# One exponential for the first half, the second half's scores earlier, and V's units regrouped in a segment-recurrent attention

## Chip, cores and metric

The kernel runs on one core of one Trainium2 chip. The metric is device time in microseconds (us) of one execution. Three runs of the kernel before gave 795.5, 796.58 and 797.68 us; the median, 796.58, is the time before.

## The reference

A gated sum of two branches over 2048 tokens of width 512, in bf16. Branch B is layer norm, a GELU layer of 1376 and a projection back. Branch A is attention over segments of 32 tokens, each with 8 memory tokens in front, 32 heads of 128; the first 8 output rows of one segment are the memory of the next, so the 64 segments are a chain:

```python
for s in range(n_seg):                       # 64
    h = jnp.concatenate([mem, x[:, 32*s:32*s+32]], axis=1)      # 40 rows
    q, k, v = (jnp.einsum('btd,dhe->bhte', h, W) for W in (Wq, Wk, Wv))
    scores = jnp.einsum('bhqe,bhke->bhqk', q, k) * scale
    p = _softmax(jnp.where(mask, scores, -1e9), axis=-1)
    o = jnp.einsum('bhqk,bhke->bhqe', p, v)
    o = jnp.einsum('bhte,hed->btd', o, Wo)
    mem = o[:, :8]
    outs.append(o[:, 8:])
return g * a + (1 - g) * b                   # g = sigmoid((x * gate_w).sum(-1))
```

## The kernel before

A first stage (lines 292 to 545, about 100 us) computes branch B and loads the weights of branch A. Then the loop of line 626 runs the 64 segments s = 4 T + si, T being a tile of 128 tokens. The order of every engine's instructions is written out by hand; nothing is rescheduled, and each engine works through its own list in order, waiting on the others by semaphores.

TensorE works in groups of four matmuls that sit side by side on the array, 32 columns each. A group with 512 columns of weights streaming past is called a unit here. hT holds the segment's input, transposed: the 8 memory rows and 24 of the segment's tokens. The remaining 8 tokens of each of the four segments of a tile ("left") have no dependence on memory and are projected one tile ahead, in side units that are spread over the segments to fill TensorE's pauses.

One segment, in TensorE's order:

1. Q and K from hT: 16 units (L110) into the PSUM banks U[0..3]; ScalarE casts each bank to Tb (L115), VectorE transposes it into QT or KT (L119). U[0] and U[1] give the first half of the heads, U[2] and U[3] the second.
2. scores of the first half (L256, L260) into the bank SbF, on top of a mask written earlier (L248). ScalarE takes the exponentials (L661) into E in two pieces: 16 of 56 columns per group, then 40. The 16 hold the memory rows' queries, the 40 the others.
3. four V units into X1 (L129), copied by ScalarE to V (L676); one V unit into X2; msum(0): the sums of the memory queries of the first half (L267, L270) into a corner of U[0]; VectorE takes the reciprocal (L668) and multiplies E by it (L669), which is mnorm(0).
4. a second V unit into X2, the scores of the second half into the bank W, their exponentials in two pieces, two more V units into X2, ScalarE's copy of X2 (L687), then msum(1) and mnorm(1).
5. `run(W1)`: W1 side units. The sums of the x queries into SbF (L267, L270 again), their reciprocal on VectorE (L603); SP writes them to memory (r_dr) and reads them back broadcast (Rb, L606, L607); GpSimd adds them to a check sum (L608).
6. A·V in two halves of the heads (L280, with L285 for the left tokens) into U; ScalarE copies the memory part to UT (L697) and the x part, raw, to XR (L598). The x part is normalised by GpSimd at the start of the next segment with Rb (L614, L615).
7. `run(W2)`: W2 side units. wo_pass: 8 units with Wo (L141) into W; ScalarE casts the result to w (L622).
8. the mask for the next segment's SbF; `run(W3)`: W3 side units; for si = 0 the output rows of tile T-2 (L226, L228), for si = 3 the transposes of x for tile T+2 (L156).
9. L709: four small matmuls pick the memory rows out of w; VectorE casts them into the next hT (L710). The side units that are left follow, then the next segment's Q and K.

A segment has at most 8 side units: left Q and K for si = 0 and 1, Wo of the left tokens for si = 2, left V for si = 3. With W1 = W2 = W3 = 2 two are left for the end. In the last tile only si = 2 has any.

Of the kernel before, what the change touches and what calls it, by code (L numbers as in the profile page):

```python
# [12 lines left out]
ACTF = mybir.ActivationFunctionType  # L13
# [14 lines left out]
def kernel(ctx, tc, A_x, A_mem0, A_Wq, A_Wk, A_Wv, A_Wo, A_seg_len, B_x, B_w1, B_b1, B_w2, B_b2, gate_w, out):  # L28
    nc = tc.nc
# [8 lines left out]
    KC = Dm // P  # L38
# [12 lines left out]
    scale = float(Dh) ** -0.5  # L51
# [35 lines left out]
    def load_xs(T):  # L87
        xs = ew.tile([P, Dm], BF16, tag="xs", name="xs")
        nc.sync.dma_start(xs[:], x2[T * P:(T + 1) * P, :])
        return xs  # L90
# [4 lines left out]
    X2 = lps.tile([P, 512], FP32)  # L95
# [3 lines left out]
    Sb = [bk[:, 0:4 * EW].rearrange("p (i c) -> p i c", c=EW) for bk in (SbF, W)]  # L99
# [7 lines left out]
    def qk_unit(bk, G, t, hf, kc):  # L107
        h0, h1 = HF[hf]
        for j in range(4):
            nc.tensor.matmul(bk[32 * j:32 * j + 32, :], lhsT=G[:, kc, :], rhs=W5[t][:, kc, h0:h1, j, :],  # L110
                             start=(kc == 0), stop=(kc == KC - 1), tile_position=(0, 32 * j))

    def qk_cast(bk):
        Tb = ew.tile([P, 8, 32, 2], BF16, tag="Tb", bufs=3, name="Tb")
        nc.scalar.copy(out=Tb[:], in_=bk.rearrange("p (a b e) -> p a e b", a=8, b=2))  # L115
        return Tb

    def qk_tr(Tb, dst, hf):
        nc.vector.transpose(out=dst[:, 8 * hf:8 * hf + 8, 0:32, :].rearrange("p a r b -> p a (r b)").bitcast(FP32),  # L119
                            in_=Tb[:].rearrange("p a e b -> p (a e b)").bitcast(FP32))  # L120
# [6 lines left out]
    def v_unit(bk, G, vb, kc):  # L127
        for j in range(4):
            nc.tensor.matmul(bk[32 * j:32 * j + 32, :], lhsT=G[:, kc, :], rhs=Wv5[:, kc, 4 * vb:4 * vb + 4, j, :],  # L129
                             start=(kc == 0), stop=(kc == KC - 1), tile_position=(0, 32 * j))  # L130

    def v_out(V, vb):
        return V[:, 4 * vb:4 * vb + 4, :].rearrange("p i e -> p (i e)")
# [15 lines left out]
    def flush(q, n=1):  # L149
        for _ in range(min(n, len(q))):  # L150
            q.pop(0)()
# [32 lines left out]
    def vp_load(T, si):  # L184
        nc.sync.dma_start(VP[T % 2][:, si].rearrange("p v e -> p (v e)"), VLs[T][si:P:SPT].rearrange("p a v e -> p a (v e)"))
# [20 lines left out]
    def c_load(T):  # L206
        c = cw.tile([P, Dm], BF16, tag="c", name="c")
        nc.sync.dma_start(c[:], c_dr[T * P:(T + 1) * P, :])
        cs[T] = c
# [27 lines left out]
    def prep_h(s):  # L237
        T, si = divmod(s, SPT)
        nc.gpsimd.tensor_copy(out=hT[s % 3][:, :, M:32], in_=xTs[T][:, :, seg * si:seg * si + RIDE])
# [6 lines left out]
    def mask_mm(i2):  # L246
        for j in range(4):
            nc.tensor.matmul(Sb[i2][32 * j:32 * j + 32], lhsT=ident[:, 32 * j:32 * j + 32], rhs=Mk[:],  # L248
                             start=True, stop=True, skip_group_check=True, tile_position=(0, 32 * j))
# [15 lines left out]
    def sums(out, E, c_main, c_left, n, start):  # L265
        for j in range(4):
            nc.tensor.matmul(out[32 * j:32 * j + 32], lhsT=BO[:, 32 * j:32 * j + 32], rhs=E[:, :, c_main:c_main + n],  # L267
                             start=start, stop=False, skip_group_check=True, tile_position=(0, 32 * j))
        for j in range(4):
            nc.tensor.matmul(out[32 * j:32 * j + 32, :, n - 8:n], lhsT=BO[:, 32 * j:32 * j + 32], rhs=E[:, :, c_left:c_left + 8],  # L270
                             start=False, stop=True, skip_group_check=True, tile_position=(0, 32 * j))
# [303 lines left out]
    def side(T, si):  # L575
        gens = []
        if si == 2:
            if T >= 1:
                gens.append(wo_left(T - 1, X1))
        elif T + 1 < NT:  # L580
            gens = [[left_qk(T + 1, 0, 0, X1), left_qk(T + 1, 1, 0, X2)], [left_qk(T + 1, 0, 1, X1), left_qk(T + 1, 1, 1, X2)], [],
                    [left_v(T + 1, 0, X1), left_v(T + 1, 1, X2)]][si]
        return chain(*gens)
# [27 lines left out]
    def x_norm(s):  # L611
        T, si = divmod(s, SPT)
        XR, Rb = XRs.pop(s)[:].rearrange("p j i q -> p (j i) q"), Rbs.pop(s)[:].rearrange("p j i q -> p (j i) q")
        nc.gpsimd.tensor_tensor(out=UT[(s + 1) % 2][:].rearrange("p j i q -> p (j i) q")[:, :, M:32], in0=XR[:, :, 0:RIDE], in1=Rb[:, :, 0:RIDE], op=ALU.mult)  # L614
        nc.gpsimd.tensor_tensor(out=UL[T % 2][:].rearrange("p j i q -> p (j i) q")[:, :, LEFT * si:LEFT * si + LEFT],  # L615
                                in0=XR[:, :, RIDE:32], in1=Rb[:, :, RIDE:32], op=ALU.mult)
# [5 lines left out]
        nc.scalar.copy(out=w[:], in_=W[:])  # L622
        return w

    W1, W2, W3 = 2, 2, 2
    for s in range(nseg):
        T, si = divmod(s, SPT)
        last = s == nseg - 1
        hc, hn = hT[s % 3], hT[(s + 1) % 3]
        fill = side(T, si)  # L630
        if s + 1 < nseg:
            prep_h(s + 1)
        if s >= 1:
            x_norm(s - 1)
        if si == 0 and T >= 2:
            c_load(T - 2)
        if si < 3:
            vp_load(T, si + 1)
        if last:
            c_load(T - 1)  # L640
            c_load(T)
        if si == 0 and T + 2 < NT:
            xss[T + 2] = load_xs(T + 2)
        for n, (t, hf) in enumerate(((0, 0), (1, 0), (0, 1), (1, 1))):
            bk = U[n]
            for kc in range(KC):
                qk_unit(bk, hc, t, hf, kc)
            if n == 0:
                flush(act_q, 9)
                mask_mm(1)  # L650
                flush(dve_q, 9)
            qk_tr(qk_cast(bk[:]), (QT, KT)[t], hf)
        V = cw.tile([P, NG, Dh], BF16, tag="V", name="V")
        E = cw.tile([P, NG, EW], BF16, tag="E", name="E")
        R = cw.tile([P, NG * 40], FP32, tag="R", name="R")
        Rs[s] = R
        xsum = SbF[:, 0:32 * NG].rearrange("p (i q) -> p i q", q=32)

        def exps(i2, x):
            c = slice(16, EW) if x else slice(0, 16)  # L660
            nc.scalar.activation(out=E[:, 4 * i2:4 * i2 + 4, c], in_=Sb[i2][:, :, c], func=ACTF.Exp, scale=scale)  # L661

        def msum(i2):
            sums(U[i2][:, 320:352].rearrange("p (i q) -> p i q", q=8), E[:, 4 * i2:4 * i2 + 4, :], 8, 0, 8, True)

        def mnorm(i2):
            r, e = R[:, 32 * i2:32 * i2 + 32], E[:, 4 * i2:4 * i2 + 4, 0:16].rearrange("p i (a q) -> p i a q", q=8)
            nc.vector.reciprocal(out=r, in_=U[i2][:, 320:352])  # L668
            nc.vector.tensor_tensor(out=e, in0=e, in1=r.rearrange("p (i q) -> p i q", q=8).unsqueeze(2).to_broadcast([P, 4, 2, 8]), op=ALU.mult)  # L669

        scores(s, 0)
        for i2 in range(2):
            exps(0, i2)
        for kc in range(KC):
            v_unit(X1, hc, 0, kc)
        nc.scalar.copy(out=v_out(V, 0), in_=X1[:])  # L676
        v_unit(X2, hc, 1, 0)
        if not last:
            msum(0)
            mnorm(0)  # L680
        v_unit(X2, hc, 1, 1)
        scores(s, 1)
        for i2 in range(2):
            exps(1, i2)
        for kc in range(2, KC):
            v_unit(X2, hc, 1, kc)
        nc.scalar.copy(out=v_out(V, 1), in_=X2[:])  # L687
        if last:
            break
        msum(1)  # L690
        mnorm(1)
        run(W1)
        sums(xsum, E, 16, 48, 32, True)
        recip_x(s)
        av(s, V, E)
        for j in (0, 2, 1, 3):
            nc.scalar.copy(out=UT[s % 2][:, j, :, 0:M], in_=U[j][:, 0:NG * 40].rearrange("p (i q) -> p i q", q=40)[:, :, 0:8])  # L697
        x_raw(s)
        run(W2)
        prep_q(s + 1)  # L700
        w = wo_pass(UT[s % 2])
        if s >= 1:
            ws[s - 1] = w
        mask_mm(0)
        run(W3)
        for _ in extra(T, si):
            pass
        for k in range(KC):
            nc.tensor.matmul(W[:, M * k:M * k + M], lhsT=w[:, k * P:(k + 1) * P], rhs=SelM[:], start=(k == 0), stop=(k == KC - 1), skip_group_check=True)  # L709
        nc.vector.tensor_copy(out=hn[:, :, 0:M], in_=W[:, 0:KC * M].rearrange("p (k m) -> p k m", k=KC))  # L710
        flush(dve_q, 9)
        nc.vector.tensor_tensor(out=rmin[:], in0=rmin[:], in1=R[:], op=ALU.min)
        for _ in fill:
            pass
        flush(act_q, 9)
# [163 lines left out]
```

## Time and profile before

| | |
|---|---|
| median of 3 runs | 796.58 us |
| profiled execution | 799.87 us |
| its span, first to last instruction | 798.1 us |
| TensorE busy (matmuls) | 774.5 us |
| ScalarE busy | 529.9 us |
| VectorE busy | 444.0 us |
| GpSimd busy | 260.4 us |

The engines are called PE (TensorE's matmuls), PEld (its weight loads), ACT (ScalarE), DVE (VectorE), POOL (GpSimd) and SP (SyncE). A row of the timeline gives the start in us from the span's start, the duration in us, engine, line, operation, out<-in, shapes and how many equal instructions follow each other; in brackets stands the engine's idle time ahead of it and what ended it. Matmuls are pipelined and overlap, so a row's duration is longer than the time until TensorE takes the next. A row of the windows gives a stretch, its length, the busy time of each engine with its instructions, the granted clock of TensorE (1.00 is full) and the DMA share. A row of the groups gives the count, then busy us and mean ns, then idle time ahead.

### The profile page before, as it was taken

To read this page: it belongs to the slowest core of one execution; us is meant where nothing else is said; L and a number is where in the kernel's file an instruction comes from. 1 tells how busy PE (TensorE), PEld (TensorE's weight loads), DVE (VectorE), ACT (ScalarE), POOL (GpSimd) and SP (SyncE) were. 2 spreads that over 40 slices of the span, in tenths; PEclk is the share of its full clock that TensorE was granted. 3 is DMA by queue.
4 is the path that set the end of the run, shared out by engine and by line. 5 is a ranking of instruction groups with operands and counts; after the bars stand their busy time and mean duration, and the time that the engine had idled before them with its cause. 6 is when DMAs were issued, how large, how long until landed. Compare 5 with 4: busy or idle time off the path is not lost.

```text
span 798.1 us, 41399 instructions
## 1 busy us (share of the span) xinstructions
PE 774.5 (97%) x18446; PEld 421.2 (53%) x18446; DVE 444.0 (56%) x1061; ACT 529.9 (66%) x1440; POOL 260.4 (33%) x391
## 2 busy tenths in 40 slices
PE   7999999999999999999999999999999999999996
PEld 5666554555555555555554555555555555555543
DVE  4776355555556454646555555655465556555554
ACT  3666676666666676666666667767666766666663
POOL 3111033333343333243343334333334333333331
PEclk9999999999999999999999999999999999999999
DMA  6779411212112222212121211222221212121211
GB/s 188 264 273 351 134 57 60 73 59 86 60 53 68 76 69 76 70 49 67 60 86 60 86 49 62 70 76 70 70 76 53 64 60 86 60 80 60 66 47 57
DMA packets 38151, 70.42 MB, mean 88 GB/s; under 512 B 3979, under 2 KB 27888, under 8 KB 36432
## 3 DMA queue, kind: packets, MB, share of 16 engines
q1 hardware_dynamic: 36448, 64.97, 24.5%
q8 instruction: 146, 2.39, 1.2%
q0 software_dynamic: 720, 1.97, 0.7%
q10 hardware_dynamic: 800, 0.79, 0.3%
q14 instruction: 37, 0.30, 0.1%
HBM read 59.06 MB, written 4.45 MB: 80 GB/s over the span
## 4 chain that ended last, share of the span: by engine, by line
PE 92%; ACT 3%; DVE 2%; issue 1%; DMA 1%; POOL 0%; DVEq 0%; POOLq 0%; ACTq 0%
PE U L110 28%; PE X L129 17%; PE W L141 14%; PE X L110 6%; PE U L468 5%; PE U L280 4%; PE X L141 3%; ACT w L622 3%; PE W L462 3%; PE SbF L462 3%; PE W L709 1%; PE U L267 1%; DVE E L669 1%; PE SbF L256 1%; PE W L248 1%
## 5 line engine op out<-in xcount | busy, mean ns | idle before, releaser
L115 ACT CAST Tb<-U 128x512 bf16<-128x512 f32 x258 | 151.2, 586 | 81.3 <-PE U L110 80.8
L614 POOL TENSOR_TENSOR UT<-XR,Rb 128x768 bf16<-128x768 bf16 x63 | 104.7, 1662 | 239.8 <-DMA Rb<-r_dr 214.6
L110 PEld LDWEIGHTS <-hT 128*32 128x32 bf16 x4096 | 103.7, 97 | 109.9 <-DVE hT L710 19.1
L110 PE MATMUL U<-Wq_sb,hT 128*32 128x512 bf16 x2048 | 132.7, 379 | 1.1 <-DVE hT L710 1.1
L129 PE MATMUL X<-Wv_sb,hT 128*32 128x512 bf16 x2048 | 133.5, 378 | 0.0
L110 PE MATMUL U<-Wk_sb,hT 128*32 128x512 bf16 x2048 | 132.7, 379 | 0.0
L141 PE MATMUL W<-Wo_sb,UT 128*32 128x512 bf16 x2080 | 124.3, 380 | 1.2 <-ACT UT L697 1.2
L608 POOL TENSOR_TENSOR racc<-racc,R 128x320 f32<-128x320 f32 x63 | 54.5, 866 | 181.1 <-DVE R L603 176.5
L603 DVE RECIPROCAL R<-SbF 128x256 f32<-128x256 f32 x63 | 110.3, 1751 | 0.0
L119 DVE STREAM_TRANSPOSE QT<-Tb 128x256 f32<-128x256 f32 x128 | 57.0, 446 | 74.2 <-ACT Tb L115 74.1
L119 DVE STREAM_TRANSPOSE KT<-Tb 128x256 f32<-128x256 f32 x128 | 57.0, 445 | 54.9 <-ACT Tb L115 54.9
L141 PEld LDWEIGHTS <-UT 128*32 128x32 bf16 x2080 | 56.3, 96 | 58.5 <-issue 20.0
L710 DVE CAST hT<-W 128x32 bf16<-128x32 f32 x63 | 12.1, 192 | 132.8 <-PE W L709 132.8
L598 ACT CAST XR<-U 128x256 bf16<-128x256 f32 x252 | 78.4, 434 | 0.0
L622 ACT CAST w<-W 128x512 bf16<-128x512 f32 x65 | 38.1, 586 | 44.8 <-PE W L141 44.8
L697 ACT CAST UT<-U 128x64 bf16<-128x64 f32 x252 | 35.3, 226 | 46.7 <-PE U L285 46.7
L668 DVE RECIPROCAL R<-U 128x32 f32<-128x32 f32 x126 | 44.9, 357 | 25.7 <-PE U L270 24.2
L129 PEld LDWEIGHTS <-hT 128*32 128x32 bf16 x2048 | 45.4, 95 | 20.6
L468 PE MATMUL U<-w_sb,hTm 128*128 128x512 bf16 (+1 forms) x176 | 53.0, 385 | 0.0
L115 ACT CAST Tb<-X 128x512 bf16<-128x512 f32 x62 | 36.5, 589 | 18.0 <-PE X L110 18.0
L462 PEld LDWEIGHTS <-w_sb 128*128 128x128 bf16 (+1 forms) x352 | 34.9, 102 | 21.4 <-issue 4.6
L267 PEld LDWEIGHTS <-BO 128*32 128x32 bf16 x760 | 26.9, 95 | 33.9 <-issue 14.5
(155 smaller groups left out, 1220.5 us busy)
## 6 DMA issues: line engine op xcount, KB each, us to landing
Rb<-r_dr SPq DMA_DIRECT2D x63, 512.0 KB
Wv_sb<-in_A_Wv_dram SPq DMA_DIRECT2D x4, 1024.0 KB
Wq_sb<-in_A_Wq_dram SPq DMA_DIRECT2D x4, 1024.0 KB
Wk_sb<-in_A_Wk_dram SPq DMA_DIRECT2D x4, 1024.0 KB
Wo_sb<-in_A_Wo_dram SPq DMA_DIRECT2D x4, 1024.0 KB
VP<-VL SPq DMA_DIRECT2D x64, 64.0 KB
xt<-in_A_x_dram SPq DMA_DIRECT2D x16, 128.0 KB
xs<-in_A_x_dram SPq DMA_DIRECT2D x16, 128.0 KB
```

The source lines that it names most:

```text
L110: nc.tensor.matmul(bk[32 * j:32 * j + 32, :], lhsT=G[:, kc, :], rhs=W5[t][:, kc, h0:h1, j, :], start=(kc == 0), stop=(kc == KC - 1), tile_ ...
L115: nc.scalar.copy(out=Tb[:], in_=bk.rearrange("p (a b e) -> p a e b", a=8, b=2))
L119: nc.vector.transpose(out=dst[:, 8 * hf:8 * hf + 8, 0:32, :].rearrange("p a r b -> p a (r b)").bitcast(FP32), in_=Tb[:].rearrange("p a e b ...
L129: nc.tensor.matmul(bk[32 * j:32 * j + 32, :], lhsT=G[:, kc, :], rhs=Wv5[:, kc, 4 * vb:4 * vb + 4, j, :], start=(kc == 0), stop=(kc == KC - ...
L141: nc.tensor.matmul(bk[32 * c:32 * c + 32, :], lhsT=U_[:, j, i, :], rhs=Wo_sb[:, 4 * i + j, :], start=(n == 0), stop=(n == NW - 1), tile_po ...
L462: nc.tensor.matmul(hp[:rows, 0:TB * P], lhsT=w1_sb[:, kc, fc * P:fc * P + rows], rhs=yTs[blk][:, kc, :], start=(kc == 0), stop=(kc == KC - 1))
L468: nc.tensor.matmul(bp(blk, tt)[:], lhsT=hTm[blk % 2][:rows, fc, tt * P:(tt + 1) * P], rhs=w2_sb[:rows, fc, :], start=(fc == 0), stop=(fc = ...
L598: nc.scalar.copy(out=XR[:, j], in_=U[j][:, 0:NG * 40].rearrange("p (i q) -> p i q", q=40)[:, :, 8:40])
L603: nc.vector.reciprocal(out=R[:, 8 * NG:], in_=SbF[:, 0:32 * NG])
L608: nc.gpsimd.tensor_tensor(out=racc[:], in0=racc[:], in1=R[:], op=ALU.add)
L614: nc.gpsimd.tensor_tensor(out=UT[(s + 1) % 2][:].rearrange("p j i q -> p (j i) q")[:, :, M:32], in0=XR[:, :, 0:RIDE], in1=Rb[:, :, 0:RIDE] ...
L622: nc.scalar.copy(out=w[:], in_=W[:])
```

## The change

```diff
-    W1, W2, W3 = 2, 2, 2
+    W1, W2, W3 = 1, 2, 3
@@
         scores(s, 0)
-        for i2 in range(2):
-            exps(0, i2)
+        nc.scalar.activation(out=E[:, 0:4, :], in_=Sb[0], func=ACTF.Exp, scale=scale)
         for kc in range(KC):
             v_unit(X1, hc, 0, kc)
         nc.scalar.copy(out=v_out(V, 0), in_=X1[:])
@@
         if not last:
             msum(0)
             mnorm(0)
-        v_unit(X2, hc, 1, 1)
         scores(s, 1)
         for i2 in range(2):
             exps(1, i2)
-        for kc in range(2, KC):
+        for kc in (1, 2):
             v_unit(X2, hc, 1, kc)
+        if not last:
+            msum(1)
+            mnorm(1)
+        v_unit(X2, hc, 1, 3)
         nc.scalar.copy(out=v_out(V, 1), in_=X2[:])
         if last:
             break
-        msum(1)
-        mnorm(1)
         run(W1)
```

The first half's exponentials become one instruction over all 56 columns. The scores of the second half move ahead of V's second unit into X2. The second sums move ahead of V's last unit, so that X2's units come as one, two and one. Of the side units one moves from behind the second sums to behind the Wo pass. The number of matmuls is the same; ScalarE has 64 instructions fewer.

## The prediction

> **What bounds the kernel now.** I read the page first, then cut the loop at each first score of a segment (windows), then one segment instruction by instruction (timeline by engine), then who waits for whom (waits). The page first:
>
> ```profile
> PE 774.5 (97%) x18446; PEld 421.2 (53%) x18446; DVE 444.0 (56%) x1061; ACT 529.9 (66%) x1440; POOL 260.4 (33%) x391
> ...
> PE 92%; ACT 3%; DVE 2%; issue 1%; DMA 1%; POOL 0%; DVEq 0%; POOLq 0%; ACTq 0%
> ```
>
> TensorE carries 92% of the chain. Its work does not change, so only its short pauses can. Stretches of one segment each (start:end, length, busy time by engine, granted clock):
>
> ```profile
> 404.82:415.68 10.86, 10.86 (x286) 5.69 (x281) 6.64 (x15) 7.57 (x22) 3.92 (x6) 1.00 0.27 87
> 415.68:426.33 10.65, 10.49 (x282) 5.47 (x277) 6.21 (x14) 7.56 (x21) 3.24 (x5) 1.00 0.16 57
> 426.33:437.83 11.50, 10.75 (x280) 5.62 (x276) 6.24 (x11) 7.07 (x20) 3.96 (x6) 1.00 0.13 51
> 230.85:242.46 11.61, 11.12 (x287) 5.85 (x282) 7.57 (x15) 7.56 (x22) 3.72 (x5) 1.00 0.31 94
> 242.46:254.11 11.65, 10.84 (x280) 5.73 (x276) 7.41 (x14) 7.58 (x21) 4.30 (x6) 1.00 0.17 56
> 361.04:372.64 11.60, 11.11 (x285) 5.85 (x281) 7.58 (x15) 7.56 (x21) 4.12 (x6) 1.00 0.27 86
> ```
>
> An ordinary segment takes 10.65 us, one that also selects output rows (si = 0) 10.86; the other four rows are disturbed (below). The clock is full throughout. Inside the segment at 415.68, TensorE first:
>
> ```profile
> 415.81 1.25 PE L129 MATMUL X<-Wv_sb,hT 128*32 128x512 bf16 x20
> 416.89 0.19 PE L267 MATMUL U<-E,BO 128*32 128x32 bf16 x4
> ...
> 416.94 0.39 PE L129 MATMUL X<-Wv_sb,hT 128*32 128x512 bf16 x4
> 417.15 0.27 PE L256 MATMUL W<-QT,KT 128*32 128x40 bf16 x16
> ...
> 417.29 0.60 PE L129 MATMUL X<-Wv_sb,hT 128*32 128x512 bf16 x8
> 417.82 0.20 PE L267 MATMUL U<-E,BO 128*32 128x32 bf16 x4
> ...
> 417.87 0.62 PE L110 MATMUL X<-Wq_sb,GL 128*32 128x512 bf16 x8
> ...
> 418.67 0.19 PE L285 MATMUL U<-E,VP 32*128 32x64 bf16 x4
> 418.84 0.28 PE L280 MATMUL U<-E,V 32*128 32x40 bf16 x16
> ...
> 421.37 0.62 PE L110 MATMUL X<-Wk_sb,GL 128*32 128x512 bf16 x8
> 422.15 0.26 PE L709 MATMUL W<-SelM,w 128*128 128x8 bf16 x4 [0.16 <-ACT w L622]
> ```
>
> Matmuls overlap, so distances between starts count, not the durations. Five V units start at 415.81 and their successor at 416.89: a unit costs 0.215 us. Two units from 417.29 would end at 417.72, but the next sums start at 417.82: a pause of 0.10. L285 needs 0.03, yet the second half of A·V (L280) starts 0.17 after it: a pause of 0.14. Two side units from 421.37 end at 421.80, L709 starts at 422.15: a pause of 0.35. What ends each is on ScalarE and VectorE:
>
> ```profile
> 415.90 0.59 ACT L115 CAST Tb<-U 128x512 bf16<-128x512 f32 x1 [0.23 <-PE U L110]
> 416.39 0.43 ACT L661 ACTIVATE E<-SbF 128x64 bf16<-128x64 f32 x2
> 416.90 0.59 ACT L676 CAST V<-X 128x512 bf16<-128x512 f32 x1
> 417.54 0.42 ACT L661 ACTIVATE E<-W 128x64 bf16<-128x64 f32 x2
> 417.94 0.59 ACT L687 CAST V<-X 128x512 bf16<-128x512 f32 x1
> ...
> 421.51 0.59 ACT L622 CAST w<-W 128x512 bf16<-128x512 f32 x1 [0.65 <-PE W L141]
> ```
>
> ```profile
> 416.52 0.45 DVE L119 STREAM_TRANSPOSE KT<-Tb 128x256 f32<-128x256 f32 x1 [0.37 <-ACT Tb L115]
> ...
> 418.56 0.23 DVE L669 TENSOR_TENSOR E<-E,R 128x64 bf16<-128x64 bf16 x1
> ```
>
> The normalised E is out at 418.56 + 0.23 = 418.79 and L280 starts at 418.84, so a released matmul follows 0.05 after its releaser. V's second copy had ended at 417.94 + 0.59 = 418.53: today V is early and E is last. The copy of w ends at 422.10, L709 follows at 422.15: w is last there.
>
> **The change part by part.**
>
> *One exponential for two.* Forms of the two, mean ns after the bar:
>
> ```profile
> L661 ACT ACTIVATE E<-SbF 128x160 bf16<-128x160 f32 x64 | 19.9, 311 | 0.0
> ...
> L661 ACT ACTIVATE E<-SbF 128x64 bf16<-128x64 f32 x64 | 14.7, 229 | 0.0
> ```
>
> The 224-column form is not in the trace. From below: 311 ns, the 160-column row. From above: 229 + 311 = 540. I take 365, by the slope between the rows, (311 - 229)/96 = 0.85 ns a column. It starts at 416.39 and ends at 416.76. The next ScalarE instruction waits for TensorE until 416.90 anyway, so the shorter work buys nothing; the first sums now wait for all of E's half, not for its 16 columns, but start only at 416.89. At 540 ns they would start 0.09 late, at 416.98, which the wait described next swallows nearly whole. Cost 0. The Trainium skill ("Perfetto Trace Analysis", section Optimizing Scalar/DVE Operations) gives ScalarE about 51 ns of overhead per instruction on PSUM and says grouping helps a saturated engine. By that the 64 merged pairs would give 3.3 us, an estimate from the page; the gap ahead of 416.90 says that ScalarE isn't the limit here, so the sum stays without it.
>
> *Scores one unit earlier.* They would start where the moved unit starts now, 416.94. But they read the K half that VectorE transposes until 416.52 + 0.45 = 416.97; plus 0.05 that is 417.02. So they come 0.13 earlier than 417.15, not 0.215, and TensorE pauses 0.08 that it didn't before. Queued behind them is all of TensorE's order; nothing on VectorE waits for it.
>
> *Exponentials of the second half* follow the scores by 417.54 - 417.15 = 0.39: 417.41. ScalarE's V copy of 416.90 allows that: after a copy of this size the next instruction started 0.49 later (415.90, 416.39), so 417.39 at the earliest. The second sums follow by 0.28: 417.69 (now 417.82). TensorE is there at 417.59, so the old 0.10 pause stays.
>
> *V's last unit behind the second sums.* It runs 417.74 to 417.96. The last unit now starts at 417.29 + 0.215 = 417.505 and its copy at 417.94, 0.44 later; so the copy now starts 418.18, ends 418.77, and the second half of A·V can start 418.82, against 418.84. E, 0.13 early, would have let it go at 418.71. So the wait changes owner, from E to V, and ends 0.02 earlier. TensorE's order between the scores and A·V has the same length as before (two units, sums, two units), so A·V's first half ends 0.13 earlier and the pause ahead of the second grows from 0.14 to 0.25. Accounts: pauses 0.08 + 0.10 + 0.25 = 0.43 against 0.24, and one unit (0.215) less done by then.
>
> *That unit, moved behind the Wo pass (1, 2, 3).* Where L709 waits for w, it fills 0.215 of the 0.35 pause, and the segment's end moves with w alone: -0.02 us. How often that is so, the waits tell (us, times, longest):
>
> ```profile
> PEld L709 <- ACT w L622: 23.8, 36, 1.0
> ```
>
> 36 of 63 segments. The other 27 have work between the side units and L709 (13 select output rows, 14 transpose x):
>
> ```profile
> 410.66 0.59 ACT L622 CAST w<-W 128x512 bf16<-128x512 f32 x1 [0.65 <-PE W L141]
> ...
> 411.51 0.24 PE L709 MATMUL W<-SelM,w 128*128 128x8 bf16 x4
> ```
>
> ```profile
> 400.01 0.59 ACT L622 CAST w<-W 128x512 bf16<-128x512 f32 x1 [0.65 <-PE W L141]
> ...
> 400.66 0.25 PE L709 MATMUL W<-SelM,w 128*128 128x8 bf16 x4
> ```
>
> w is out at 411.25, 0.26 before L709, and at 400.60, just before it. There the moved unit stands in front of L709 and pushes the next segment's input by its whole length: 0.215 - 0.02 = +0.195. The two units after L709, which cover the way back to hT, stay two. So 27 x 0.195 = +5.3 us, 36 x -0.02 = -0.7 us.
>
> *Moved with it.* The x sums come 0.13 earlier, and with them the reciprocal, both SP transfers of r_dr and Rb and GpSimd's work on R; none is passed by another on SP or POOL, and nothing on the chain waits for them except here:
>
> ```profile
> 427.93 1.65 POOL L614 TENSOR_TENSOR UT<-XR,Rb 128x768 bf16<-128x768 bf16 x1 [5.90 <-DMA Rb<-r_dr]
> ```
>
> ```profile
> 428.34 1.32 DVE L669 TENSOR_TENSOR E<-E,R 128x64 bf16<-128x64 bf16 x1
> ```
>
> When Rb lands late, GpSimd's multiply lies over VectorE's small one, which takes 1.32 us instead of 0.23 and ends 0.08 behind it. That makes the four long segments: 0.85 + 0.75 + 1.00 + 0.74 = 3.3 us. The Trainium skill ("SBUF — State Buffer", section SBUF: two separate sides) calls the port that GpSimd and VectorE share an exclusive lock held for a whole instruction; the 1.32 us row agrees. With the sums 0.13 earlier and 27 segments 0.195 longer, GpSimd starts some 0.1 to 0.3 us earlier against VectorE's instruction, so each such case shrinks by that much: with the same four about -0.8 us. Landings vary; bounds are -3.3 (all gone) and +1 (one more). I take -0.8.
>
> **Sum:** 5.3 - 0.7 - 0.8 = +3.8 us on the profiled execution's 799.87. The median of the runs is 796.58, 0.4% lower; the terms are per segment, so I add them unscaled: 800.4 us, +0.5%. Rows have two decimals; 0.03 us per segment is 1.9 us of the sum.
>
> **Rivals.**
> - *Faster: V's copy isn't last.* If the copy starts 0.11 sooner after its unit than the row says, E releases A·V's second half at 418.71, 0.13 earlier. Then 36 x -0.13 + 27 x 0.085 - 0.8 = -3.2: 793.4. For it: the third unit does fit w's pause. Against: 0.44 from unit to copy, and both copies are bound to TensorE. It decides where the copy ends before 418.66. Chance 0.08.
> - *GpSimd's overlap goes altogether.* 5.3 - 0.7 - 3.3 = +1.3: 797.9, within 0.3%. For: all four need a late landing. Against: a shift of 0.1 to 0.3 does not clear overlaps of a microsecond. Chance 0.16.
> - *ScalarE doesn't start the exponentials early.* The V copy ends at 417.49, and 417.54 is 0.05 after that too. If the exponentials wait for its end rather than for the scores, they stay at 417.54, the last V unit starts at 417.87, its copy ends at 418.90, A·V's second half starts at 418.95: 36 x 0.11 + 27 x 0.325 - 0.8 = +11.9: 808.5. Against: 415.90 and 416.39 overlap. Chance 0.08.
>
> **How the numbers follow.** My case has 0.64, with 797.9 to 803 as its own range from the rounding and the overlap's bounds; 0.04 is left for anything else. The range 796.5 to 805 leaves out the first and the last rival. A measurement here tells about 0.3%, 2.4 us, so no change reaches from 794.2 to 799.0. Faster: 0.08 and 0.01 of the rest. Same: 0.16, less 0.02 of it that ends higher, plus 0.12 of my case. Slower: the remaining 0.65.
>
> **What would show it.** In the profile after: the second scores 0.05 behind the K transposition; V's second copy, not E, ahead of A·V's second half; si = 1 and 2 segments still at about 10.63 with L709 waiting for w some 0.14; si = 0 at 11.05 and si = 3 at 10.84. Wrong if A·V's second half moves by more than 0.05, if si = 0 and 3 are not some 0.2 longer, or if VectorE's small multiply is stretched in more segments than now.

## The result, and the profile after

The changed kernel takes 801.76 us (median of 6 runs, 799.76 to 802.39) against 796.74 us for the kernel before (6 runs): a ratio of 1.0064, 95% interval 1.005 to 1.0078, so 4.0 to 6.2 us slower. I had forecast 800.4, within 796.5 to 805.0. The profiled execution took 802.39 us with a span of 800.6. One of the 12 runs of a kernel further down, the new order with the old side units, took 1274.96 us at a granted clock of 0.56; it counts in that kernel's median and not in its ratio.

The page of the kernel after, the lines that answer to those shown of before:

```profile
PE 774.2 (97%) x18417; PEld 425.2 (53%) x18446; DVE 441.6 (55%) x1061; ACT 522.6 (65%) x1376; POOL 260.5 (33%) x391
...
PE 89%; ACT 7%; DVE 1%; issue 1%; DMA 1%; POOL 0%; DVEq 0%; POOLq 0%; ACTq 0%
PE U L110 28%; PE X L129 17%; PE W L141 14%; PE X L110 6%; PE U L468 5%; ACT V L689 4%; PE X L141 3%; PE W L462 3%; PE SbF L462 3%; PE U L280 2%; PE W L709 1%; PE W L256 1%; ACT Tb L115 1%; PE U L267 1%; PE SbF L256 1%
```

TensorE's work is the same, but ScalarE's share of the chain went from 3% to 7%, and 4% of the span is one line that wasn't among the chain's lines before: L689, V's second copy. The stretches from one first score to the next, in the windows of after:

```profile
393.44:404.29 10.85, 10.76 (x285) 5.77 (x281) 5.54 (x12) 7.46 (x21) 4.10 (x7) 1.00 0.22 70
404.29:415.34 11.05, 10.80 (x285) 5.83 (x281) 6.64 (x15) 7.45 (x20) 3.66 (x6) 1.00 0.28 87
415.34:425.97 10.63, 10.54 (x280) 5.56 (x276) 6.22 (x14) 7.45 (x20) 3.10 (x5) 1.00 0.19 57
425.97:437.84 11.87, 10.77 (x280) 5.72 (x276) 6.61 (x11) 6.95 (x19) 3.96 (x6) 1.00 0.16 50
```

They are si = 3, 0, 1 and a disturbed si = 2. The segment at 415.34 again, TensorE, ScalarE and VectorE:

```profile
416.57 0.19 PE L270 MATMUL U<-E,BO 128*32 128x32 bf16 x4
416.68 0.28 PE L256 MATMUL W<-QT,KT 128*32 128x40 bf16 x16
...
417.34 0.20 PE L267 MATMUL U<-E,BO 128*32 128x32 bf16 x4
417.37 0.20 PE L270 MATMUL U<-E,BO 128*32 128x32 bf16 x4
417.40 0.40 PE L129 MATMUL X<-Wv_sb,hT 128*32 128x512 bf16 x4
...
418.19 0.19 PE L285 MATMUL U<-E,VP 32*128 32x64 bf16 x4
418.48 0.27 PE L280 MATMUL U<-E,V 32*128 32x40 bf16 x16
```

```profile
416.05 0.36 ACT L672 ACTIVATE E<-SbF 128x224 bf16<-128x224 f32 x1
416.56 0.59 ACT L675 CAST V<-X 128x512 bf16<-128x512 f32 x1
417.07 0.42 ACT L661 ACTIVATE E<-W 128x64 bf16<-128x64 f32 x2
417.84 0.59 ACT L689 CAST V<-X 128x512 bf16<-128x512 f32 x1 [0.35 <-PE X L129]
```

```profile
416.18 0.45 DVE L119 STREAM_TRANSPOSE KT<-Tb 128x256 f32<-128x256 f32 x1 [0.37 <-ACT Tb L115]
...
417.62 0.36 DVE L668 RECIPROCAL R<-U 128x32 f32<-128x32 f32 x1
418.09 0.23 DVE L669 TENSOR_TENSOR E<-E,R 128x64 bf16<-128x64 bf16 x1
```

K's transposition ends at 416.63 and the second scores start at 416.68, not at some 416.60, where TensorE was free (an estimate: the row of sums at 416.57 and the 0.03 that lie between such a row and its successor at 417.37 and 417.40). V's last unit starts at 417.40, its copy 0.44 later; it ends at 418.43, and A·V's second half starts at 418.48. E was out at 418.32. So V's copy is last here, where E was before. The waits (us, times, longest) say it for the whole run:

```profile
PEld L709 <- ACT w L622: 16.7, 36, 1.0
...
PEld L280 <- ACT V L689: 12.0, 58, 0.3
```

A·V waits for V's copy in 58 of 63 segments. L709 still waits for w in the same 36, 7.1 us less in all (23.8 before): that is what the third side unit filled, and none of it reached the end.

### The profile page after: what moved, and what is told of

It is laid out like the page before. It is cut to its first block, busy times and chain, and to the rows that moved or that the text cites. A ratio compares the mean times of both kernels' runs of the same rounds, so it can differ in the third digit from the quotient of the medians.

```text
span 800.6 us, 41349 instructions
## 1 busy us (share of the span) xinstructions
PE 774.2 (97%) x18417; PEld 425.2 (53%) x18446; DVE 441.6 (55%) x1061; ACT 522.6 (65%) x1376; POOL 260.5 (33%) x391
## 4 chain that ended last, share of the span: by engine, by line
PE 89%; ACT 7%; DVE 1%; issue 1%; DMA 1%; POOL 0%; DVEq 0%; POOLq 0%; ACTq 0%
PE U L110 28%; PE X L129 17%; PE W L141 14%; PE X L110 6%; PE U L468 5%; ACT V L689 4%; PE X L141 3%; PE W L462 3%; PE SbF L462 3%; PE U L280 2%; PE W L709 1%; PE W L256 1%; ACT Tb L115 1%; PE U L267 1%; PE SbF L256 1%
## 5 line engine op out<-in xcount | busy, mean ns | idle before, releaser
L614 POOL TENSOR_TENSOR UT<-XR,Rb 128x768 bf16<-128x768 bf16 x63 | 104.7, 1662 | 236.9 <-DMA Rb<-r_dr 182.6
L129 PE MATMUL X<-Wv_sb,hT 128*32 128x512 bf16 x2048 | 142.3, 378 | 0.0
L689 ACT CAST V<-X 128x512 bf16<-128x512 f32 x64 | 37.5, 586 | 22.7 <-PE X L129 22.7
L267 PEld LDWEIGHTS <-BO 128*32 128x32 bf16 x760 | 32.2, 94 | 35.1 <-issue 13.4
L468 PE MATMUL U<-w_sb,hTm 128*128 128x512 bf16 (+1 forms) x163 | 49.8, 383 | 0.6
```

Of the source, the lines that this page charges most:

```text
L468: nc.tensor.matmul(bp(blk, tt)[:], lhsT=hTm[blk % 2][:rows, fc, tt * P:(tt + 1) * P], rhs=w2_sb[:rows, fc, :], start=(fc == 0), stop=(fc = ...
```

## The experiments

Theory A is the prediction's: only the wait that ends last ahead of A·V, of L709 and of the next hT counts; a side unit is free where such a wait covers it and costs its length elsewhere. So the loss is the side unit pushed in front of L709 in 27 segments, and the new order of scores and V is worth almost nothing, slightly for the better. Theory B, the rival: the regrouping of V is the loss, since it makes V's copy late, and the third unit behind Wo pays in the 36 segments.

**The merged exponential alone** (kernel before otherwise):

```diff
-        for i2 in range(2):
-            exps(0, i2)
+        nc.scalar.activation(out=E[:, 0:4, :], in_=Sb[0], func=ACTF.Exp, scale=scale)
```

> Only the merged exponential; everything else as before. Theory A (only the wait that ends last ahead of A·V, of L709 and of hT counts): ScalarE waits for TensorE behind these exponentials either way, so 0, 796.7 us within 1 us, steady segments still 10.65 us (si = 1, 2, 3) and 10.85 (si = 0). Theory B (regrouping V costs, the third side unit behind Wo pays): 0 too. If the merged form held up the first sums, segments would be up to 0.09 us longer: 802.

Measured 796.02 us against 796.62, ratio 0.9997 (0.9986 to 1.0007). It costs and gains nothing that can be told from these runs, which leave room for 1 us either way.

**The side units alone** (kernel before otherwise):

```diff
-    W1, W2, W3 = 2, 2, 2
+    W1, W2, W3 = 1, 2, 3
```

> Only W1, W2, W3 = 1, 2, 3; exponentials, scores and V units as before. Theory A: E stays last ahead of A·V's second half at the same time, so the unit taken from there leaves a pause of its own length; behind Wo it fills a pause in 36 segments (0 change, 10.65 us) and pushes L709 in 27 (+0.215 us each: si = 0 at 11.07, si = 3 at 10.86). Sum 27 x 0.215 = +5.8: 802.5 us. Theory B: 36 segments gain 0.215 us, 27 lose nothing: 789; or, if the 27 lose as in A, 795.

Measured 802.85 us, ratio 1.0076 (1.0061 to 1.0091): +6.2 us, as A said. Its windows show si = 3, 0, 1:

```profile
393.20:404.06 10.86, 10.84 (x284) 5.84 (x280) 5.54 (x12) 7.56 (x22) 4.63 (x7) 1.00 0.21 71
404.06:415.13 11.07, 10.89 (x284) 5.86 (x281) 6.64 (x15) 7.56 (x22) 3.63 (x6) 1.00 0.26 86
415.13:425.78 10.65, 10.63 (x280) 5.62 (x276) 6.20 (x14) 7.56 (x21) 2.95 (x5) 1.00 0.17 60
```

The two kinds of segment that have other work ahead of L709 are 0.21 to 0.22 longer than before (10.65 and 10.85), the third kind stands at 10.65. In that last row TensorE is busy for 10.63 us where it was busy for 10.49 before: busier, and no shorter. B is out in its main claim.

**The new order with the old side units** (changed kernel otherwise):

```diff
-    W1, W2, W3 = 1, 2, 3
+    W1, W2, W3 = 2, 2, 2
```

> The changed kernel with W1, W2, W3 put back to 2, 2, 2: the merged exponential, the earlier scores and V's units in one, two, one stay. Theory A: V's copy still is last ahead of A·V's second half, about 0.02 us earlier than E was before, and nothing is pushed in front of L709: all segments 0.02 us shorter (10.63 us; si = 0 10.84), 63 x 0.02 = -1.1: 795.6 us. Theory B: the regrouping is the loss, so the loss stays or grows: 802 to 808 us.

Measured 794.82 us, ratio 0.9978 (0.9969 to 0.9987): faster than both kernels. Windows, si = 3, 0, 1:

```profile
389.70:400.33 10.63, 10.63 (x284) 5.76 (x280) 5.63 (x12) 7.44 (x21) 3.77 (x7) 1.00 0.24 71
400.33:411.17 10.84, 10.68 (x284) 5.76 (x281) 6.74 (x15) 7.45 (x21) 3.88 (x6) 1.00 0.29 89
411.17:421.81 10.64, 10.48 (x282) 5.55 (x277) 6.31 (x14) 7.45 (x20) 3.45 (x5) 1.00 0.18 60
```

Each segment is 0.02 shorter, 1.1 us over 63; the interval (0.13 to 0.31%) allows 1.0 to 2.5. So the whole loss of the change goes away with the one line of side units.

**One, two, three only where L709 waits for w** (changed kernel otherwise):

```diff
         fill = side(T, si)
+        W1, W2, W3 = (1, 2, 3) if si in (1, 2) else (2, 2, 2)
```

> The changed kernel with 1, 2, 3 for si = 1 and 2 alone, and 2, 2, 2 for si = 0 and 3. Theory A: the third unit only swaps one pause for another where L709 waits for w, so the same as with 2, 2, 2 throughout: 795.6 us, si = 1 and 2 at 10.63 us either way. Theory B: some 31 segments gain up to 0.215 us against 2, 2, 2 throughout: 6.7 us less than that kernel.

Measured 795.61 us, ratio 0.9990 (0.9981 to 1.0000). Its si = 1 segment:

```profile
412.42:423.05 10.63, 10.55 (x280) 5.55 (x276) 6.32 (x14) 7.44 (x20) 3.72 (x5) 1.00 0.18 58
```

10.63, as with 2, 2, 2 in the run above (10.64 in its row). The 6.7 us that B expected aren't there; the third unit swaps one pause for another.

**V's second copy early, from another bank** (changed kernel otherwise; V's second half then holds numbers of K's projection, so the output isn't the reference's):

```diff
             exps(1, i2)
+        nc.scalar.copy(out=v_out(V, 1), in_=U[3][:])
...
-        nc.scalar.copy(out=v_out(V, 1), in_=X2[:])
```

> The changed kernel (1, 2, 3), but ScalarE's second V copy reads the bank U[3], which is long done, right behind the exponentials, and not X2: V's second half then holds other numbers, the amount of work is the same. Theory A: V's copy no longer is last ahead of A·V's second half; E is, at 418.09 + 0.23 + 0.05 = 418.37 in the changed kernel's profiled segment, against 418.48, so every segment is 0.11 us shorter: 63 x 0.11 = 7 us below the changed kernel's 801.8, 794.8; si = 1, 2 at 10.52, si = 0 at 10.94, si = 3 at 10.73. Rival: if the copy isn't what is waited for, 801.8 stays.

Measured 796.25 us, 5.5 below the changed kernel's median (expected 7). Windows, si = 3, 0, 1:

```profile
391.40:402.13 10.73, 10.73 (x285) 5.78 (x281) 5.53 (x12) 7.34 (x21) 4.30 (x7) 1.00 0.24 74
402.13:413.06 10.93, 10.93 (x285) 5.78 (x281) 6.64 (x15) 7.34 (x20) 3.52 (x6) 1.00 0.24 84
413.06:423.58 10.52, 10.52 (x281) 5.58 (x277) 6.21 (x14) 7.34 (x20) 3.48 (x5) 1.00 0.21 58
```

Every kind of segment is 0.11 to 0.12 shorter than in the changed kernel; E's earlier time gives 0.11. So V's copy was last, by that much.

**X2's three units in a row, sums behind them** (2, 2, 2, early scores):

```diff
-        for kc in (1, 2):
+        for kc in (1, 2, 3):
             v_unit(X2, hc, 1, kc)
         if not last:
             msum(1)
             mnorm(1)
-        v_unit(X2, hc, 1, 3)
```

> Side units 2, 2, 2, the scores as early as in the changed kernel, but X2's three units in a row behind them and the sums behind these. Theory A: V's copy is early again and E last: scores 1.34 us into the segment, 0.13 for them, three units 0.645: sums at 2.12, E 0.74 + 0.23 + 0.05 behind: 3.14 us, against 3.165 before and 3.14 in the changed kernel. So 0.02 to 0.03 us a segment below before, like the kernel with 2, 2, 2 and the changed order: 795 us. Rival: if the regrouping as such costs, this is 2 us or more off that kernel.

Measured 799.35 us, ratio 1.0021 (1.0008 to 1.0035). The number expected was 795. The steady segment is 0.03 longer than before, not shorter (windows, si = 1):

```profile
414.11:424.79 10.68, 10.49 (x280) 5.63 (x276) 6.29 (x14) 7.45 (x20) 3.68 (x5) 1.00 0.20 58
```

E is last again, as expected, but later than worked out. In a segment of this kernel the sums start at 459.78 and the reciprocal at 460.10 (timeline):

```profile
457.64 0.27 PE L256 MATMUL SbF<-QT,KT 128*32 128x40 bf16 x16
...
459.78 0.19 PE L267 MATMUL U<-E,BO 128*32 128x32 bf16 x4
```

```profile
460.10 0.36 DVE L668 RECIPROCAL R<-U 128x32 f32<-128x32 f32 x1 [0.20 <-PE U L270]
460.56 0.23 DVE L669 TENSOR_TENSOR E<-E,R 128x64 bf16<-128x64 bf16 x1
```

That is 0.32 us, where both other kernels have 0.28 (417.34 to 417.62 in the changed kernel; 417.82 to 418.10 in the kernel before). It is 0.32 in 50 of the 63 segments here, and 0.28 in 53 and 51 of them there. There TensorE had paused ahead of the sums; here it streamed a unit right up to them. That this is the reason was not tested. The sums themselves start at 2.14 us into the segment, not 2.12, so that E is ready at 460.56 + 0.23 + 0.05 - 457.64 = 3.20 us, against 3.14 expected.

**V's last unit in two halves** (2, 2, 2, early scores), one ahead of the sums, in the pause, one behind; v_half is v_unit on 256 of the 512 columns:

```diff
         for kc in (1, 2):
             v_unit(X2, hc, 1, kc)
+        v_half(X2, hc, 1, 3, 0)
         if not last:
             msum(1)
             mnorm(1)
-        v_unit(X2, hc, 1, 3)
+        v_half(X2, hc, 1, 3, 1)
```

> Side units 2, 2, 2 and the changed order, with V's last unit cut in two: 256 columns ahead of the second sums, where TensorE pauses 0.10 us for the exponentials, and 256 behind them. Theory A: V's copy starts 0.107 us sooner and E's time stays, so that both are done 3.03 us into the segment, against 3.165 before: 63 x 0.13 = 8 us below before, 788.5 us, segments of 10.52 us (si = 0: 10.72). Rival: TensorE's order, not the two late inputs, sets A·V; then it stays at 795 us, or loses some for four more small matmuls a segment.

Measured 794.58 us, ratio 0.9962 (0.9950 to 0.9974): 3 us and not 8 below before. It has the lowest median here, though its interval overlaps with that of the new order with 2, 2, 2 (0.9969 to 0.9987). Steady segments, si = 0 and si = 1:

```profile
401.72:412.47 10.75, 10.75 (x291) 5.93 (x286) 6.71 (x15) 7.45 (x21) 3.35 (x5) 1.00 0.30 90
499.01:509.56 10.55, 10.39 (x285) 5.63 (x280) 6.28 (x14) 7.45 (x20) 3.49 (x6) 1.00 0.19 59
```

Both are some 0.10 below before, by the segment starts 6.4 us over 63; 0.13 a segment were expected. In the si = 0 segment the two late inputs, V's copy and E, and A·V's second half:

```profile
404.13 0.59 ACT L695 CAST V<-X 128x512 bf16<-128x512 f32 x1 [0.26 <-PE X L134]
```

```profile
404.50 0.23 DVE L674 TENSOR_TENSOR E<-E,R 128x64 bf16<-128x64 bf16 x1
```

```profile
404.78 0.28 PE L285 MATMUL U<-E,V 32*128 32x40 bf16 x16
```

Both inputs are out within 0.01 of each other, and A·V's second half (L285 here) follows 3.06 us into the segment, not 3.03: the sums start at 403.74, right behind the half unit of 403.63, which is 2.02 into the segment against 2.00 in the changed kernel, and E and the other half unit follow from there.

The rest of the gain was taken back by disturbed segments. I added up, over the 63 segments of each profiled execution, what lies above that kernel's own steady lengths, by the segment starts: 5.3 us before, 3.6 after, 8.4 here, and 1.1 in the run with 2, 2, 2 above. The mean of VectorE's small multiply (0.226 us undisturbed) moves the same way; the group's row of before, of after, of this kernel and of the one with 2, 2, 2:

```profile
L669 DVE TENSOR_TENSOR E<-E,R 128x64 bf16<-128x64 bf16 x126 | 36.2, 287 | 13.5 <-ACT V L687 0.5
```

```profile
L669 DVE TENSOR_TENSOR E<-E,R 128x64 bf16<-128x64 bf16 x126 | 33.6, 267 | 13.5 <-ACT V L689 0.5
```

```profile
L674 DVE TENSOR_TENSOR E<-E,R 128x64 bf16<-128x64 bf16 x126 | 38.2, 303 | 13.5 <-ACT V L695 0.5
```

```profile
L669 DVE TENSOR_TENSOR E<-E,R 128x64 bf16<-128x64 bf16 x126 | 30.5, 242 | 13.5 <-ACT V L689 0.5
```

In these four traces every small multiply that takes over 0.3 us ends 0.08 to 0.09 us behind the end of one of GpSimd's two multiplies, the large one into UT or the smaller one behind it into UL (0.676 us). The smaller one is the more frequent: 9 of 14 before, 18 of 24 here. Segments with such a multiply hold 4.5 of the 5.3 us before and 6.4 of the 8.4 here.

**GpSimd's large multiply, into UT, in four pieces**, in three kernels; the smaller one into UL stays whole:

```diff
-        nc.gpsimd.tensor_tensor(out=UT[(s + 1) % 2][:].rearrange("p j i q -> p (j i) q")[:, :, M:32], in0=XR[:, :, 0:RIDE], in1=Rb[:, :, 0:RIDE], op=ALU.mult)
+        for j in range(4):
+            nc.gpsimd.tensor_tensor(out=UT[(s + 1) % 2][:, j, :, M:32], in0=XR[:, NG * j:NG * j + NG, 0:RIDE], in1=Rb[:, NG * j:NG * j + NG, 0:RIDE], op=ALU.mult)
```

> The kernel before, with GpSimd's multiply into UT in four instructions, one per j, in place of one of 1.66 us. Overlap theory: VectorE's small multiply then waits for a piece of some 0.4 to 0.5 us at the most, the segments of 11.5 us and more go, and of the some 4 us that VectorE's stretched multiplies cost in the profiled execution 2 to 3 go: 794 us; steady segments stay at 10.65 and 10.85. Rival: the long segments come from somewhere else, or GpSimd, slower by its four starts, is late for Wo: 796.7 or more.

> The changed kernel with GpSimd's multiply into UT in four pieces. Overlap theory: it had less of the overlap than the kernel before (two segments near 12 us in the profiled execution), so 1 to 2 us less than 801.8: 800 us; steady segments 10.63, 11.05 (si = 0), 10.84 (si = 3). Rival: no difference, 801.8.

> V's last unit in two halves around the second sums, side units 2, 2, 2, and GpSimd's multiply into UT in four pieces. Overlap theory: with one multiply, shorter segments brought GpSimd's work closer to VectorE's (7.4 us above the steady segments in the profiled execution), and that ate most of the 6.4 us that the steady segments gained; in pieces 3 to 4 us of it come back: 791 us. Rival: the rest is not GpSimd's doing: 794.6 stays.

Measured against the kernel before, at 796.51 in these rounds: before in pieces 799.81, ratio 1.0045 (1.0028 to 1.0062); after in pieces 802.55, 1.0071 (1.0056 to 1.0086), no different from the changed kernel's 1.0064; split in pieces 798.95, 1.0033 (1.0018 to 1.0047), against 0.9962. So this cure fails. GpSimd's two multiplies, in the kernel before and in its version in pieces, and there VectorE's small multiply (groups):

```profile
L614 POOL TENSOR_TENSOR UT<-XR,Rb 128x768 bf16<-128x768 bf16 x63 | 104.7, 1662 | 239.8 <-DMA Rb<-r_dr 214.6 <-ACT Tb L115 25.3
```

```profile
L615 POOL TENSOR_TENSOR UT<-XR,Rb 128x192 bf16<-128x192 bf16 x252 | 131.8, 556 | 242.0 <-DMA Rb<-r_dr 224.1 <-ACT E L662 9.0 <-ACT Tb L115 8.8
...
L670 DVE TENSOR_TENSOR E<-E,R 128x64 bf16<-128x64 bf16 x126 | 43.4, 345 | 13.5 <-ACT V L688 0.5
L616 POOL TENSOR_TENSOR UL<-XR,Rb 128x256 bf16<-128x256 bf16 x63 | 42.6, 676 | 0.0
```

A piece takes 556 ns, four of them 2.22 us in place of 1.66. No small multiply of VectorE is stretched beyond 1 us any more (4 were), but 37 are beyond 0.4 us (13 were), and the mean rises from 287 to 345 ns. Of those 37, only 9 end behind a piece and 28 behind the multiply into UL, which the edit left whole and which now comes some 0.56 us later (2.22 less 1.66). That the longest small multiply shrank with the longest instruction of GpSimd, from 1.48 to 0.71 us, agrees with the Trainium skill ("SBUF — State Buffer", section SBUF: two separate sides), by which the shared port stays locked for a whole instruction. But where the 3.3 us between the medians come from isn't shown: the two profiled executions, 799.87 and 799.2, don't differ that way, since that of before lies 3 us above its own median. And no run cut both multiplies or took the overlap away, so its share of the medians stays open.

## Why the prediction was right

*The merged exponential at 0.* Right, by itself (ratio 0.9997) and in size: 363 ns (0.36 in the row) against 365 estimated.

*Scores 0.13 earlier, held by K.* Right: 0.05 behind the transposition; 1.34 us into the segment, against 1.47 before.

*A·V's second half handed from E to V's copy, 0.02 earlier.* Right: 418.48 - 415.34 = 3.14 us into the segment, against 418.84 - 415.68 = 3.16. The early copy (run with U[3]) shows that V held it, the run with 2, 2, 2 that the new order is worth those 0.02 a segment. The copy's end, 418.43, is 3.09 us into the segment, as worked out (418.77 - 415.68).

*The side unit behind Wo.* Right, and the core of it: but for the disturbed ones, 36 segments take 10.63, 13 take 11.05 and 14 take 10.84 or 10.85 (the forecast had 10.63, 11.05 and 10.84). By the segment starts, 13 x 0.197 + 14 x 0.193 - 36 x 0.017 = +4.65 us, against 5.3 - 0.7 = +4.6 forecast. Side units alone cost 6.2 us, the new order gives back 1.8.

*GpSimd's overlap at -0.8.* This term did not come out in the median: +5.0 us measured less 4.65 steady leaves +0.4, with an interval of about 1.1 either way. Between the two profiled executions the disturbed segments did give back more than taken, 5.3 to 3.6 us (the prediction's 3.3 counts the four longest alone), and these two differ by only 2.5 us (799.87, 802.39). But the forecast took its four cases from an execution that was 3 us above the median it was added to, and the runs of the kernel before lie between 794.65 and 798.98 us, which is wider than the term. 0 would have been the better value for a forecast of the median, and 801.2 the forecast. In the profile after, the small multiply took over 0.4 us 9 times, against 13 before.

Of the rivals, the late ScalarE is refuted by the row at 417.07, which starts while the copy of 416.56 still runs (to 417.15). The faster one failed on the 0.44 us from unit to copy. And GpSimd's overlap did not go altogether; two small multiplies still took over a microsecond, this one the longest (timeline of after):

```profile
427.99 1.70 DVE L669 TENSOR_TENSOR E<-E,R 128x64 bf16<-128x64 bf16 x1
```

## What to carry to other kernels

Work that is moved into a pause gains nothing if the place it leaves becomes a pause of the same length, because something else holds the next step there. So write down, for each wait, which input ends last and by how much the next one follows, and check in which iterations of the loop the new place is a pause at all. Here it was one in 36 of 63 segments and in front of the critical result in the other 27. A chain that is bound by latency gets shorter where the two last inputs are both brought forward, as the halved V unit did. Then the next thing in line can take part of the gain back; in that profile it was the segments in which VectorE's multiply lay over one of GpSimd's.

## What the runs showed of the hardware

The time from a TensorE group to the engine that reads it isn't a constant: from the second sums to their reciprocal 0.28 us where TensorE had paused ahead of them, 0.32 where it came straight from a 512-column unit. A small multiply of VectorE that lay over one of GpSimd's multiplies took up to 1.70 us in place of 0.226 and ended 0.08 to 0.09 us behind GpSimd's. And GpSimd's multiply pays some 0.19 us for each extra instruction (4 x 556 against 1662 ns, over three).
